# Linear attention before two feed-forward layers: k products on row halves, zero products in front, and two smaller edits in the first eight pairs

## The chip, the cores and the metric

The kernel runs on one core of one Trainium2 chip. The metric is the device time of one execution in microseconds (us); lower is better. Engines are called as in the profile: PE (TensorE products) and PEld (its weight loads), DVE (VectorE), ACT (ScalarE), POOL (GpSimd), SP (SyncE, which here only issues DMAs).

## The reference, cut to what matters

```python
def phi(x):
    proj = np.einsum('bhsd,df->bhsf', x, w_phi)
    proj = proj - np.max(np.abs(proj), axis=-1, keepdims=True)
    return np.concatenate([np.exp(proj), np.exp(-proj)], axis=-1)
q_p, k_p = (phi(q), phi(k))
kv = np.einsum('bhsf,bhsd->bhfd', k_p, v)
z = np.sum(k_p, axis=2)
num = np.einsum('bhsf,bhfd->bhsd', q_p, kv)
den = np.einsum('bhsf,bhf->bhs', q_p, z)[..., None] + 1e-06
attn = num / den
```

There are 4 batches, 8 heads, 576 positions, a head width of 64 and 128 features. The attention's output, 2304 tokens by 512, then goes through two feed-forward layers (512 to 2048 to 512), the first with a leaky ReLU and the second with SiLU.

## The kernel before, in words

Heads are worked in 16 pairs (4 for each batch). Head 0 of a pair lies on rows 0 to 63 of a tile, head 1 on rows 64 to 127. The first eight pairs (`full(i)`, `NFULL` = 8) use plain f32 products, the other eight split operands. Before the first feed-forward layer begins, the kernel does nearly all of the first eight pairs' work; the second eight are woven into that layer.

Steps of one of the first eight pairs, by line:

- L115 to L117 and L123: SP issues the loads of k (`kr`, 512 positions), of k's last 64 positions of both heads (`kt`), of q (`qr`) and of v (`va`).
- L180 (`s_pk(0)` and `s_pk(1)`): k times phi's weights. The 128 rows of a 128-position block of k are the weights in the array, and a block-diagonal matrix `BDF` (128 x 256) runs through it, so that one product gives both heads' 128 features. Each of the four blocks is one product, and each f32 product is two instructions with a weight load each: 8 instructions a pair. Two blocks fill one PSUM bank (`ps_a`, four of them).
- L156, L157 (`k_features`): DVE takes the largest absolute value of each of the four groups in a bank, and subtracts it. L166, L167: ACT takes exp of the negative (`ke[:, :, 1]`), and then, in place, exp (`ke[:, :, 0]`), once for the first bank (512 columns) and once for the second together with the tail (640).
- L195: the same product for the tail. L217: q's products, on row halves already: head j uses rows 64 j to 64 j + 63 of `qr` and of `wraw`, and writes to a bank of its own. ACT copies them out (L223, L225), POOL takes the largest absolute value over the partitions (L227).
- L262, L268 (`s_kv`): exp features times v, 18 products (36 instructions) into one bank, sign 0 first, then sign 1. ACT copies the sums out (L273, tile `KV`, one buffer).
- L302, L305: q's features times `KV`; DVE divides (L311 to L313); L316, L320: transposes; ACT and DVE split the result into `xh` and `xl` (L287, L126), the operands of the feed-forward layer (L533, L553).

`wc` holds `BDF` in columns 0 to 255, and `wraw` (w_phi on both row halves) and the identity in columns 256 to 511. ACT's queue issues it as two DMAs (L75), `BDF` first.

Beside this, the feed-forward weights come from 64-bit words: SP loads `raw` (L411; three buffers, and some loads held back until POOL has written a token of a given pair), ACT and DVE narrow and split it (L420 to L425, L429, L126), and the second matrix is stored again (L485). The written order comes from the table `OFF0` (a due time for each step of a pair) with five units between pairs. From it the framework plans the order on each engine, with its own estimates of durations; the order in the profile is not quite the written one. On the chip each engine then runs its instructions strictly in that order, SP's queue too.

Of the kernel before, what the change touches and what calls it, by code (L numbers as in the profile page):

```python
# [8 lines left out]
F32 = mybir.dt.float32  # L9
# [10 lines left out]
def tile_linear_attention_ffn_ffn(ctx: ExitStack, tc: tile.TileContext, q, k, v, w_phi, w_in1, w_out1, w_in2, w_out2, out):  # L20


    nc = tc.nc
    B, H, S, D = 4, 8, 576, 64
    F = (w_phi.shape[1] - 128) // 3
# [5 lines left out]
    S0 = 512  # L31
# [6 lines left out]
    NKV, NNUM = 112, 96  # L38
# [5 lines left out]
    gp = ctx.enter_context(tc.tile_pool(name="gp", bufs=2))  # L44
# [7 lines left out]
    def at(shape, dt, tag):  # L52
        return att_pool[0].tile(shape, dt, tag=tag, bufs=AB[0].get(tag, 1), name=tag)

    def ps(tag):

        return psp.tile([128, 512], F32, tag=tag, name=f"ps_{tag}")
# [3 lines left out]
    def aps(step):  # L61

        return ps("y" if PRO[0] and step in ("pq", "kv", "nt") else "a")
# [3 lines left out]
    BDF, wraw, ident = wc[:, 0 : 2 * F].rearrange("p (j f) -> p j f", j=2), wc[:, 2 * F : 3 * F], wc[:, 3 * F :]  # L67
# [5 lines left out]
    def make_consts():  # L73
        for c in (slice(0, 2 * F), slice(2 * F, 3 * F + 128)):
            nc.scalar.dma_start(wc[:, c], w_phi[:, c])  # L75
        first = [const.tile([128, 2], F32, name=f"first{i}") for i in range(2)]
        nc.gpsimd.memset(first[0], 0.0)
        nc.gpsimd.partition_all_reduce(first[1], first[0], 128, bass_isa.ReduceOp.absmax)
# [30 lines left out]
    def load_qk(i):  # L109

        st = P[i]
        st["kr"] = at([128, S0], F32, "kr")
        st["kt"] = at([128, 128], F32, "kt")
        st["qr"] = at([128, S], F32, "qr")
        nc.sync.dma_start(st["kr"], k[i, :, 0:S0])  # L115
        nc.sync.dma_start(st["kt"], k[i, :, S0:])
        nc.sync.dma_start(st["qr"], q[i])  # L117

# [6 lines left out]
    def sub(out_, x, h):  # L125
        nc.vector.tensor_tensor(out_, x, h.bitcast(F32), op=ALU.subtract)  # L126

    def full(i):
        return i < NFULL
# [21 lines left out]
    def k_features(i, pk, ng, g0):  # L151

        ke = P[i]["ke"]
        km = at([128, 4], F32, "km")
        src = pk[:, 0 : ng * F].rearrange("p (g f) -> p g f", f=F)
        nc.vector.tensor_reduce(km[:, 0:ng], src, op=ALU.max, axis=AX.X, apply_absolute_value=True)  # L156
        nc.vector.tensor_tensor(  # L157
            ke[:, g0 : g0 + ng, 0, :], src, km[:, 0:ng].unsqueeze(2).to_broadcast([128, ng, F]), op=ALU.subtract
        )
        g1 = g0 + ng  # L160
        if g1 == 8:
            return
        if g1 == 9:
            g0 = 4
        e0, e1 = ke[:, g0:g1, 0, :], ke[:, g0:g1, 1, :]
        nc.scalar.activation(e1, e0, AF.Exp, scale=-1.0)  # L166
        nc.scalar.activation(e0, e0, AF.Exp)  # L167

    def s_pk(c2):
        def f(i):  # L170
            st = P[i]
            if c2 == 0:
                st["ke"] = at([128, 9, 2, F], F32, "ke")
            pk = aps("pk")
            for u in range(2):
                c = 2 * c2 + u
                cs = slice(c * 128, (c + 1) * 128)
                o = pk[:, u * 2 * F : (u + 1) * 2 * F]
                if full(i):
                    nc.tensor.matmul(o, st["kr"][:, cs], BDF.rearrange("p j f -> p (j f)"), start=True, stop=True)  # L180
                    continue
                bh, bl = BDH.rearrange("p j f -> p (j f)"), BDL.rearrange("p j f -> p (j f)")
                nc.tensor.matmul(o, st["krh"][:, cs], bh, start=True, stop=False)
                nc.tensor.matmul(o, st["krl"][:, cs], bh, start=False, stop=False)
                nc.tensor.matmul(o, st["krh"][:, cs], bl, start=False, stop=True)
            k_features(i, pk, 4, 4 * c2)

        return f
# [67 lines left out]
    def s_kv(i):  # L256
        st = P[i]
        ke, va = st["ke"], st["va"]
        pv = aps("kv")[:, 0 : 4 * NKV].rearrange("p (s j d) -> p s j d", s=2, j=2)
        vf = va.rearrange("p c d -> p (c d)")  # L260
        for s in range(2):
            nc.tensor.matmul(  # L262
                pv[:, s, :, 0 : D + 1], ke[:, 8, s, :], va[:, 8:10], start=True, stop=False, skip_group_check=True
            )
            for j in range(2):
                for c in range(4):
                    w = (4 * j + c) * (D + 1)
                    nc.tensor.matmul(  # L268
                        pv[:, s, j], ke[:, 2 * c + j, s, :], vf[:, w : w + NKV], start=False, stop=(j == 1 and c == 3), skip_group_check=True
                    )  # L270
        if full(i):
            st["KV"] = at([128, 2, 2, NNUM], F32, "KV")
            nc.scalar.activation(st["KV"], pv[:, :, :, 0 : NNUM], AF.Copy)  # L273
            return
        h, l = st["KVH"], st["KVL"] = at([128, 2, 2, 2, D], F32R, "KVH"), at([128, 2, 2, 2, D], F32R, "KVL")
        for j in range(2):
            kv_, z_ = pv[:, :, j, 0:D], pv[:, :, j, D : D + 1].to_broadcast([128, 2, D])
            for slot, sr in ((j, kv_), (1 - j, z_)):
                nc.scalar.activation(h[:, j, :, slot, :], sr, AF.Copy)
                sub(l[:, j, :, slot, :], sr, h[:, j, :, slot, :])  # L280
# [80 lines left out]
    def s_num(a):  # L361
        return lambda i: (num_full if full(i) else num_split)(i, a)

    W, WP = 8.0, 5.0
    fns = dict(
        lq=load_qk, lv=load_v, sp=s_split, pq0=s_pq(0), pq1=s_pq(1),
        pk0=s_pk(0), pk1=s_pk(1), pkt=s_pkt, eq0=s_eq(0), eq1=s_eq(1), kv=s_kv, num0=s_num(0), num1=s_num(1), fin0=s_fin(0), fin1=s_fin(1),
    )
    FIN = 16
# [19 lines left out]
    def run_att(until, tile_=None):  # L389
        while seq and (seq[-1][0] < until or (tile_ is not None and missing(tile_))):  # L390
            if seq[-1][1] == NFULL and AB[0] is ABUFS0:
                att0_ctx.close()
                att_pool[0] = att_ctx.enter_context(tc.tile_pool(name="att1", bufs=1))
                AB[0] = ABUFS1
            _, i, n_ = seq.pop()
            f = fns[n_]
            f(i)
# [76 lines left out]
    def prep_wi(layer, c):  # L474
        raw = load_wi(layer, c)
        h = wp.tile([128, KD, 128], F32R, tag="wih", bufs=NC, name="wih")
        l = wp.tile([128, KD, 128], F32R, tag="wil", bufs=NC, name="wil")
        split64(raw, h.rearrange("p k f -> p (k f)"), l.rearrange("p k f -> p (k f)"))
        wi[layer, c] = (h, l)
# [235 lines left out]
    def pace(s):  # L715

        return SLOW * min(s, NC) + FAST * max(0, s - NC)

    make_consts()
    for c in range(PRE):  # L720
        run_att(13.52 + 11.07 * c)
        prep_wi(0, c)
# [52 lines left out]
    for u, gs in GROUPS.items():  # L775
        for i, ps_ in enumerate(gs):
# [7 lines left out]
            if last:  # L784
                y = y3_ops(u, list(ps_))
# [87 lines left out]
```

## Time and profile before

| | us |
|---|---|
| median of 3 runs | 964.19 (962.32 to 964.91) |
| the profiled execution's own time | 963.19 |
| its span, first to last instruction | 961.4 |
| PE busy | 943.6 (98%) |
| DVE busy | 649.1 (68%) |
| ACT busy | 597.2 (62%) |

The span is 1.8 us less than the profiled execution's time; the rest lies around it. A busy PE is one with some product in flight, so its share does not say how fast products follow each other. The clock column of the profile reads full speed from start to end.

### The profile page before, as it was taken

The numbers are of one execution on the slowest core, as the hardware profiler recorded it, in microseconds if no ns is written. First come the engines' busy times: TensorE is split into PE (matmuls) and PEld (weight loads), VectorE is DVE, ScalarE is ACT, GpSimd is POOL, SyncE is SP. The second block draws the span as 40 slices with busy tenths as digits, with TensorE's granted clock in tenths as the row PEclk, the third lists the DMA queues.
The fourth block names the chain that finished last, engine by engine and source line by source line (L and its number), as shares of the span: only waits on it lengthen the run. The fifth ranks groups of instructions, "written<-read, shape, count | busy, mean of one in ns | idle before, by whom it ended". The sixth has DMA issues, their size and how long they took to land.

```text
span 961.4 us, 15778 instructions
## 1 busy us (share of the span) xinstructions
PE 943.6 (98%) x5376; PEld 883.6 (92%) x5376; DVE 649.1 (68%) x1279; ACT 597.2 (62%) x1224; POOL 78.4 (8%) x56
## 2 busy tenths in 40 slices
PE   7999999999999999999999999999999999999998
PEld 6878888889999998888888999999999999999998
DVE  6677799986666655278777767778762595624853
ACT  6568687877777776466655556566554565544553
POOL 3434200201111111000000000000000000000000
PEclk9999999999999999999999999999999999999999
DMA  6333477874334232299999999896988778987784
GB/s 223 99 105 102 154 243 256 284 267 129 116 112 116 78 128 79 86 355 384 356 337 334 368 356 346 299 349 239 319 287 294 243 234 264 300 281 222 251 278 138
DMA packets 102384, 226.13 MB, mean 235 GB/s; under 512 B 15008, under 2 KB 24992, under 8 KB 102304
## 3 DMA queue, kind: packets, MB, share of 16 engines
q1 hardware_dynamic: 102016, 224.86, 69.9%
q8 instruction: 43, 0.70, 0.3%
q14 instruction: 37, 0.30, 0.1%
q10 hardware_dynamic: 288, 0.26, 0.1%
HBM read 177.82 MB, written 47.22 MB: 234 GB/s over the span
## 4 chain that ended last, share of the span: by engine, by line
PE 79%; DMA 8%; DVE 6%; ACT 4%; issue 1%; SPq 1%; DVEq 0%; ACTq 0%
PE ps_y L689 18%; PE ps_y L553 16%; PE ps_a L533 16%; PE ps_a L613 10%; PE ps_y L613 8%; DMA d<-rec 2%; PE ps_a L268 2%; PE ps_a L302 2%; DMA rec<-e 2%; PE ps_a L334 1%; PE ps_y L268 1%; DMA raw<-in_moe_w_in_dram 1%; DMA e<-d 1%; PE ps_a L180 1%; DMA w7s<-wst 1%
## 5 line engine op out<-in xcount | busy, mean ns | idle before, releaser
L689 PE MATMUL ps_y<-gt,ws 128*128 128x384 f32 x1008 | 177.2, 337 | 0.0
L689 PEld LDWEIGHTS ps_y<-gt,ws 128*128 128x128 f32 x1008 | 176.4, 188 | 0.1
L553 PE MATMUL ps_y<-gh,wo 128*128 128x460 f32 (+1 forms) x640 | 149.5, 372 | 2.2 <-DVE wo L126 1.3
L553 PEld LDWEIGHTS ps_y<-gh,wo 128*128 128x128 f32 x640 | 119.0, 188 | 16.6 <-ACT gh L429 1.9
L533 PE MATMUL ps_a<-xh,wih 128*128 128x460 f32 (+1 forms) x320 | 119.4, 373 | 0.8 <-ACT p L223 0.8
L533 PE MATMUL ps_a<-xl,wih 128*128 128x460 f32 (+1 forms) x320 | 118.9, 372 | 0.0
L533 PE MATMUL ps_a<-xh,wil 128*128 128x460 f32 (+1 forms) x320 | 118.7, 371 | 0.0
L613 PE MATMUL ps_a<-xs,ws 128*128 128x384 f32 x546 | 104.7, 338 | 0.1
L613 PEld LDWEIGHTS ps_a<-xs,ws 128*128 128x128 f32 x546 | 96.7, 188 | 0.8 <-issue 0.4
L227 POOL PARTITION_ALL_REDUCE m<-p x32 | 72.9, 2280 | 293.7 <-ACT p L223 212.4
L429 ACT ACTIVATE gt<-g 128x384 fp32r<-128x384 f32 x120 | 62.8, 524 | 51.3 <-PE ps_y L689 49.3
L126 DVE TENSOR_TENSOR gt<-g,gt 128x384 fp32r<-128x384 f32 x120 | 66.5, 555 | 34.4 <-ACT gt L429 33.5
L613 PE MATMUL ps_y<-xs,ws 128*128 128x384 f32 x462 | 88.5, 338 | 0.1
L613 PEld LDWEIGHTS ps_y<-xs,ws 128*128 128x128 f32 x462 | 81.7, 188 | 0.6 <-DVE g L589 0.5
L553 PE MATMUL ps_y<-gl,wo 128*128 128x460 f32 (+1 forms) x320 | 81.6, 372 | 0.0
L126 DVE TENSOR_TENSOR gl<-g,gh 128x460 fp32r<-128x460 f32 (+1 forms) x80 | 51.6, 646 | 30.6 <-ACT gh L429 26.1
L533 PEld LDWEIGHTS ps_a<-xh,wih 128*128 128x128 f32 x320 | 60.2, 188 | 7.4 <-ACT p L223 1.0
L553 PEld LDWEIGHTS ps_y<-gl,wo 128*128 128x128 f32 x320 | 60.2, 188 | 7.0
L536 ACT ACTIVATE g<-ps_a 128x460 f32<-128x460 f32 (+1 forms) x80 | 44.1, 552 | 35.9 <-PE ps_a L533 35.1
L533 PEld LDWEIGHTS ps_a<-xh,wil 128*128 128x128 f32 x320 | 60.1, 188 | 6.8
L533 PEld LDWEIGHTS ps_a<-xl,wih 128*128 128x128 f32 x320 | 60.2, 188 | 6.0
L429 ACT ACTIVATE gh<-g 128x460 fp32r<-128x460 f32 (+1 forms) x80 | 46.6, 584 | 8.1 <-PE ps_y L553 7.1
(142 smaller groups left out, 1552.3 us busy)
## 6 DMA issues: line engine op xcount, KB each, us to landing
ws<-w7s SPq DMA_DIRECT2D x336, 256.0 KB, 3.7
wo<-wos SPq DMA_DIRECT2D x64, 512.0 KB, 5.2
w7s<-wst SPq DMA_DIRECT2D x48, 512.0 KB, 6.0
raw<-in_moe_w_in_dram SPq DMA_DIRECT2D x32, 512.0 KB, 5.3
raw<-in_moe_w_out_dram SPq DMA_DIRECT2D x32, 512.0 KB, 5.8
wos<-wo SPq DMA_DIRECT2D x16, 512.0 KB, 4.3
va<-in_v_dram SPq DMA_DIRECT2D x16, 325.0 KB, 4.1
qr<-in_q_dram SPq DMA_DIRECT2D x16, 288.0 KB, 3.9
```

The source lines that it names most:

```text
L126: nc.vector.tensor_tensor(out_, x, h.bitcast(F32), op=ALU.subtract)
L180: nc.tensor.matmul(o, st["kr"][:, cs], BDF.rearrange("p j f -> p (j f)"), start=True, stop=True)
L227: nc.gpsimd.partition_all_reduce(m, p, 128, bass_isa.ReduceOp.absmax)
L268: nc.tensor.matmul(pv[:, s, j], ke[:, 2 * c + j, s, :], vf[:, w : w + NKV], start=False, stop=(j == 1 and c == 3), skip_group_check=True)
L302: nc.tensor.matmul(pb[:, w : w + NNUM], e[:, s, cs], KV[:, s, j], start=(s == 0), stop=(s == 1))
L334: nc.tensor.matmul(o, lhs, st[m, a][:, s, j * w : (j + 1) * w], start=(n == 0), stop=(n == 5))
L429: nc.scalar.activation(h, f, AF.Copy)
L533: nc.tensor.matmul(ph, a[:, kk, :], b_[:, kk, :], start=(m == 0), stop=(m == 3 * KD - 1))
L536: nc.scalar.activation(g, ph, AF.Prelu, alpha=0.01)
L553: nc.tensor.matmul(Y[t][d][:, 0:n], a[:, ds_], b_, start=(c == 0 and m == 0), stop=(c == NC - 1 and m == 1), skip_group_check=True)
L613: nc.tensor.matmul(bank[b_], w[:, a, kk], x[:, c, kk], start=(first and m == 0), stop=(m == 5), skip_group_check=True)
L689: nc.tensor.matmul(bank[b_][db], w[:, a, db], t[:, c], start=(first and p == 0 and m == 0), stop=(p == NP - 1 and m == 2), skip_group_chec ...
```

## The change

Four edits. (1) In the first eight pairs, k's products are made head by head on row halves: the weights are 64 rows of k, and `wraw`'s 64 rows (128 columns) run through, so that a pair takes 8 products (16 instructions and 16 weight loads) where it took 4 (8 and 8). A bank holds one head's four blocks instead of two blocks of both heads, and both banks are asked for before the first product. `k_features` then runs on both, one after the other; the index of `ke` in `s_kv` follows. (2) A zeroed tile and three products on it stand ahead of the attention. (3) The first pair's `kr` comes as two DMAs. (4) `s_kv` begins with sign 1, whose exp ACT writes first.

```diff
-        nc.sync.dma_start(st["kr"], k[i, :, 0:S0])
+        for c in (slice(0, 256), slice(256, S0)) if i == 0 else (slice(0, S0),):
+            nc.sync.dma_start(st["kr"][:, c], k[i, :, c])
...
+            if full(i):
+                if c2 == 0:
+                    pks = [aps("pk"), aps("pk")]
+                    for c in range(4):
+                        for j in range(2):
+                            r = slice(64 * j, 64 * j + 64)
+                            nc.tensor.matmul(
+                                pks[j][:, c * F : (c + 1) * F], st["kr"][r, c * 128 : (c + 1) * 128], wraw[r], start=True, stop=True
+                            )
+                    for j in range(2):
+                        k_features(i, pks[j], 4, 4 * j)
+                return
...
-                if full(i):
-                    nc.tensor.matmul(o, st["kr"][:, cs], BDF.rearrange("p j f -> p (j f)"), start=True, stop=True)
-                    continue
...
-        for s in range(2):
+        for s in (1, 0):
...
+                    g = 4 * j + c if full(i) else 2 * c + j
                     nc.tensor.matmul(
-                        pv[:, s, j], ke[:, 2 * c + j, s, :], vf[:, w : w + NKV], start=False, stop=(j == 1 and c == 3), skip_group_check=True
+                        pv[:, s, j], ke[:, g, s, :], vf[:, w : w + NKV], start=False, stop=(j == 1 and c == 3), skip_group_check=True
...
+    def wake():
+
+        z, bank = gp.tile([128, 256], F32, tag="g", name="z", bufs=2), ps("y")
+        nc.vector.memset(z, 0.0)
+        for _ in range(3):
+            nc.tensor.matmul(bank[:, 0:256], z[:, 0:128], z, start=True, stop=True)
+
     make_consts()
+    wake()
```

## Rows read from the trace of the kernel before

**Rows 1.** The page's part 1: busy us, share of the span, instructions.
```profile
PE 943.6 (98%) x5376; PEld 883.6 (92%) x5376; DVE 649.1 (68%) x1279; ACT 597.2 (62%) x1224; POOL 78.4 (8%) x56
```

**Rows 2.** Windows of the attention's stage: stretch, length, busy of each engine, PEclk, DMA share, GB/s.
```profile
0.00:18.20 18.20, 12.29 (x67) 9.80 (x67) 10.43 (x19) 11.09 (x23) 5.10 (x9) 1.00 0.81 276
18.20:72.00 53.80, 51.71 (x387) 44.39 (x387) 40.45 (x84) 34.84 (x80) 20.64 (x16) 1.00 0.33 97
72.00:98.50 26.50, 25.46 (x198) 21.97 (x196) 21.16 (x50) 20.71 (x47) 11.12 (x10) 1.00 0.30 100
```

**Rows 3.** Chain of work that ended last, 0 to 24 us: start, us, what.
```profile
0.72 3.54 DMA wc<-in_w_phi_dram
4.30 3.80 PE ps_a L180 x8
...
8.49 5.30 DMA raw<-in_moe_w_in_dram
...
13.81 0.68 ACT t L420
...
22.48 2.00 PE ps_a L302 x16
```

**Rows 4.** Timeline: start, us, engine, line, shapes, count [idle before, releaser].
```profile
0.72 0.39 SPq L115 DMA_DIRECT2D kr<-in_k_dram  x1
4.73 0.31 ACT L81 ACTIVATE WH<-wc 128x128 fp32r<-128x128 f32 x1
8.12 0.69 DVE L156 TENSOR_REDUCE km<-ps_a 128x4 f32<-128x512 f32 x1 [0.29 <-PE ps_a L180]
12.10 0.49 PE L262 MATMUL ps_y<-va,ke 128*128 128x130 f32 x2 [0.43 <-ACT ke L167]
17.63 0.49 ACT L273 ACTIVATE KV<-ps_y 128x384 f32<-128x384 f32 x1
18.17 2.02 PE L302 MATMUL ps_a<-KV,qh 128*128 128x96 f32 x16 [1.17 <-ACT KV L273]
90.22 0.41 PE L316 MATMUL ps_y<-wc,x 128*128 128x128 f32 x2 [0.80 <-DVE x L313]
104.99 0.49 PE L262 MATMUL ps_y<-va,ke 128*128 128x130 f32 x2 [0.36 <-ACT ke L167]
```

**Rows 5.** Chain of work that ended last, 25 to 50 us: PE's blocks.
```profile
25.17 0.74 PE ps_y L217 x4
...
30.11 0.63 PE ps_y L217 x4
...
33.58 1.73 PE ps_a L180 x8
...
36.27 0.42 PE ps_y L262 x2
36.69 1.77 PE ps_y L268 x16
38.46 0.24 PE ps_y L262 x2
...
46.39 0.87 PE ps_a L180 x4
...
47.73 1.06 PE ps_a L180 x4
```

**Rows 6.** Chain of work that ended last, 61 to 98.5 us.
```profile
61.10 0.17 DVE d L311
...
71.92 3.84 DMA raw<-in_moe_w_out_dram
...
83.65 4.34 DMA raw<-in_moe_w_in_dram
...
98.01 0.48 DVE x L313
```

**Rows 7.** Line 75, the two loads of `wc`: issue to landing.
```profile
DMA to landing us min/median/max: 3.5/3.6/3.6
```

## The prediction

> **What bounds the kernel now.** I read the page's totals first: PE is busy 98% of the span [rows 1], so time is won only where PE gets less work or waits less. All four edits lie in the stage of the first eight pairs, which ends where the feed-forward layer begins, near 112 us; so I cut it by windows next [rows 2]. The reader should see three different stretches. To 18.2 us PE works 12.29 us, and the DMA engines are 0.81 busy at 276 GB/s. To 72 us PE is busy 51.71 of 53.80. To 98.5 us it is busy 25.46 of 26.50, but DVE works 21.16 there. Then I followed the chain of waits to see which of them ends each stretch.
>
> To 22.5 us the chain is weights of phi, first k products, the load of `raw`, then ACT and DVE without a pause until PE's next block [rows 3]. ACT stands still until that load has landed at 13.79 (8.49 + 5.30); `KV`, behind it in ACT's order, comes at 17.63, and PE's block at 18.17 has waited 1.17 us for it [rows 4]. From 22.5 to 61 us the chain is nearly all PE; pieces of it are in [rows 5]. From 61.10 it leaves PE for DVE and ACT, goes through two loads of feed-forward weights, of which the second is issued only when the first has been worked through, and comes back from DVE at 98.01 + 0.48 [rows 6]. PE stays busy beside that, and shows once how close DVE is: 0.80 us at 90.22 [rows 4].
>
> **k products on row halves.** What goes is 8 instructions in 1.73 us, 0.216 each for 256 columns [rows 5]. What comes is 16 instructions of 128 columns, so 0.108 each by column count. The nearest row for products this short is v's: 16 in 1.77 us, 0.111 each, with a weight load apiece [rows 5]. Whether two row halves run beside each other is shown by q's products, which are laid out so already: four instructions of 256 columns take 0.63 us, of 320 columns 0.74 [rows 5]. One after the other they would take 4 x 0.216 = 0.86. As two steps of two they take 2 x 0.216 = 0.43 and 0.20 more; with 320 columns 2 x 0.27 = 0.54 and 0.20 more. So halves overlap, and 0.20 is what entering this layout costs. Leaving it costs the next block 0.18: the first two of a kv group take 0.42 behind q's products and 0.24 otherwise [rows 5]. The new block is therefore 0.20 + 8 x 0.111 + 0.18 = 1.27 us, 0.46 less than 1.73. Bounds: with no overlap 16 x 0.111 + 0.38 = 2.16, 0.43 more than now; next to q's products, where both changes of layout fall away, 0.89, so 0.84 less. I take 0.46, since pairs 2 to 7 have other products around k's now. In pairs 4 and 5 the eight instructions are cut in two by the transposes, 0.87 + 1.06 [rows 5]; asking for both banks at once makes them one block, and saves 0.66.
>
> A bank a head: DVE's first reduction of 0.69 us now starts when half of the products are done and the second waits for the rest (0.29 us in the first pair [rows 4]); afterwards both can start after 0.20 + 0.89 us instead of 0.87 and 1.73. DVE needs about 2.8 us for both halves either way (two reductions and two subtractions of 0.69), so this is 0.2 us later at one end and nothing on the path. The number and shapes of DVE's and ACT's instructions do not change.
>
> **The first pair and the zero products.** The 8 first products take 3.80 us where later ones take 1.73 [rows 3, 5]; the clock column reads 1.00 here too [rows 2], so I go by the durations, which fit half speed (1.2 against 2.4 GHz) in the first products PE does at all. Three zero products are six instructions of the same shape, 6 x 0.475 = 2.9 us at that speed, and one small DVE write ahead of them. They lie in PE's 4.30 us of waiting for `wc` [rows 3], so they cost nothing as long as `wc` lands after about 4 us. If they raise the clock, the first k block is some 1.1 to 1.3 us instead of 3.8.
>
> Against that, the new products read `wraw`, which is in the second load of `wc`: issued at 1.15 us and landing 3.5 to 3.6 us later [rows 7], so near 4.7; ACT's copy of it starts at 4.73 [rows 4]. PE starts 0.45 us later, and k in halves can't help, since k has landed by 4.3. The second half of k is one issue more on SP (0.39 [rows 4]), ahead of `kt`, q and v of this pair and all loads behind; the DMA engines are loaded through this stretch [rows 2], so I let it cost nothing; without that cover it is 0.4.
>
> What is that worth? PE reaches the second pair's k about 2 us earlier, but ACT still waits for `raw` at 13.79. That landing is set by the bytes queued ahead, not by PE. I expect one exp of pair 1 (0.52 to 0.6 us) to move ahead of that wait, and so 0.5 us at 18.17 [rows 4]. Bounds: nothing (or 0.45 later), and 1.17, all of PE's wait there.
>
> **Sign 1 first.** kv waits for the second exp at 12.10 (0.43) and at 104.99 (0.36) [rows 4]; with sign 1 first the exp that is needed ends one exp, over 0.6 us, earlier, and the other is needed only 18 products of 0.111 later. The first wait is covered by ACT's wait for `raw`; the second counts: 0.36.
>
> **The sum.** Pair 2's 0.46 at 20 us falls away, since PE is released at 22.48 by ACT and DVE [rows 3]. Pairs 3 and 4 count, 0.46 + 0.66 = 1.12. Pair 5's block is at 61 us, just where the chain leaves PE: I count half, 0.33. Pairs 6 and 7, at 75 and 87 us, only make PE wait longer for DVE [rows 6], so 0. With 0.5 from the start and 0.36 from the sign: 2.3 us. The profiled execution took 963.19, so 960.9; the median of the runs shown is 1.0 above it, and for it I forecast 964.19 - 2.3 = **961.9**, 0.24% less. A measurement of this kernel tells about 0.3% (2.9 us) from no change, so this is on the edge. Its own range, with the start between +0.45 and -1.17 and pair 5 whole or not at all: 960.9 to 963.2.
>
> **Rivals.**
> PE counts everywhere. For it: from 18.2 to 72 us PE is busy 96%, and the loads on the chain wait on an order that is planned anew for the changed program. Then 1.17 + 4 x 0.46 + 2 x 0.66 + 0.36 = 4.7 us, so 959.5; where k comes next to q in some pairs, up to 0.38 more for each. Against it: rows 6, 27 us without PE.
>
> Slower: the eight steps don't reach 0.111 us. A step with 16 instructions and 16 weight loads on halves is in no row; q's steps are twice as long, and v's have one weight load, not two at once. If the weights of a half can't be loaded under that half's own products, a step is load and product one after the other, 0.111 (v's step, which a load can't exceed) + 0.108 = 0.219, and the block is 8 x 0.219 + 0.38 = 2.13, 0.40 more than now. The change loses from a step of (1.73 - 0.38) / 8 = 0.169 on. With 0.40 in pairs 1 to 7 and 0.45 at the start: 0.45 + 7 x 0.40 = 3.25 us, so 967.4. Against it: q's four instructions have room for one exposed load only (0.20), not for two. By itself: the Trainium skill, "TensorE: Matmul & The Clock Gate", section "Part 3: Packing small matmuls", says that a weight load overlaps products in flight only where the row group differs; by that rule the slower time would come out, but on the full array v's 0.111 a step, load included, already disagrees with it.
>
> It does nothing: all of PE's savings are swallowed by ACT, DVE and loads, and only the 0.36 stays: 963.8, within 0.3%. For it: the chain is off PE for 22 + 37 of 112 us.
>
> **How the numbers follow.** Forecast 0.39, PE everywhere 0.37, does nothing 0.11, slower by the steps 0.09, and 0.04 for a newly planned order that costs elsewhere. Faster by over 0.3%: 0.37 and the forecast's lower end, 0.42. Within 0.3%: the rest of the forecast and "nothing", 0.45. Slower: 0.13. The range goes from 958.2, within the rival where PE counts everywhere, to 965.5; it leaves out the slower cases and the far end of the faster one, some 0.2.
>
> **What would show it.** In the timeline of the changed kernel: zero products done before 4 us; first k product near 4.7 (right: `wraw` gates); its 16 instructions within 1.3 us (the clock is up) or 2.2 (it is not). Later k blocks of about 1.27 us in the chain, in pairs of starts; 2.1 would be the slower rival. `raw` landing near 13.8 again, and PE's block after `KV` within 0.5 to 1.2 us of 18.17. PE waits for DVE between 75 and 98.5 growing by about a microsecond (forecast), or not (PE everywhere). First feed-forward product near 109.7 instead of 112, and all later stages shifted by as much. A shift that the feed-forward stages lose or add to would prove me wrong where I looked least.

## The result and the profile after

The changed kernel takes 977.35 us (median of 4 runs, 975.51 to 978.11) against 964.25 for the kernel before (962.32 to 964.91): a ratio of 1.0136, 95% interval 1.0116 to 1.0157. The forecast was 961.9, and the range ended at 965.5. The profiled execution took 977.40 with a span of 975.6, 14.2 more than the 961.4 of before.

Read the page's totals first, as before: PE's instructions and busy time, then the clock in 40 slices of 24 us.

```profile
PE 956.5 (98%) x5446; PEld 894.4 (92%) x5446; DVE 649.6 (67%) x1280; ACT 595.4 (61%) x1224; POOL 75.6 (8%) x56
...
PEclk9879999999999999999999999999999999999999
```

PE is as busy as before by its share [rows 1], although its k products are shorter; but the second and third slices are below full clock. So the windows of [rows 2] come next, of the changed kernel, and with them the two stretches in which its granted-clock record reads half.

```profile
0.00:18.20 18.20, 15.12 (x89) 12.25 (x90) 9.96 (x17) 11.41 (x24) 6.51 (x9) 1.00 0.80 269
18.20:72.00 53.80, 48.52 (x314) 40.81 (x315) 32.43 (x66) 26.82 (x60) 15.22 (x14) 0.81 0.26 78
72.00:98.50 26.50, 25.58 (x214) 22.11 (x213) 21.08 (x46) 18.46 (x43) 9.97 (x9) 1.00 0.31 97
...
24.00:30.80 6.80, 6.80 (x30) 5.51 (x29) 3.44 (x9) 4.73 (x12) 2.34 (x1) 0.50 0.15 43
51.30:65.00 13.70, 13.12 (x58) 10.74 (x56) 6.26 (x15) 6.39 (x16) 1.05 (x1) 0.50 0.29 85
```

The same two stretches of the kernel before:

```profile
24.00:30.80 6.80, 6.80 (x56) 5.75 (x55) 3.31 (x8) 3.73 (x10) 2.34 (x1) 1.00 0.22 62
51.30:65.00 13.70, 13.12 (x94) 10.82 (x92) 9.52 (x21) 8.65 (x20) 4.96 (x4) 1.00 0.31 89
```

In 20.5 us PE is busy 19.92 us in both kernels, with 88 instructions in the changed kernel and 150 in the kernel before. Half speed (1.2 GHz instead of 2.4) cannot be seen in a busy share; it shows in the clock column and in the counts. As an estimate, half of the 20.5 us, it accounts for some 10 us.

The first feed-forward product stands at 125.1 us (before 111.7), so 13.4 of the 14.2 us are lost in the first eight pairs. (The prediction places all four edits there; the fourth, sign 1 first, also changes the second eight pairs, and the other 0.8 us were not followed up.) Where in that stage? The timeline of the changed kernel, answering to [rows 4]:

```profile
1.17 2.93 PE L735 MATMUL ps_y<-z 128*128 128x256 f32 x6 [1.17 <-DVE z L733]
4.28 0.31 ACT L81 ACTIVATE WH<-wc 128x128 fp32r<-128x128 f32 x1 [0.20 <-DMA wc<-in_w_phi_dram]
...
17.50 0.49 ACT L284 ACTIVATE KV<-ps_y 128x384 f32<-128x384 f32 x1
18.05 2.02 PE L313 MATMUL ps_a<-KV,qh 128*128 128x96 f32 x16 [1.44 <-ACT KV L284]
18.29 0.68 DVE L436 CUSTOM_DVE_ANT_0 r<-t,r 128x1024 uint16<-128x1024 uint16 x1
...
19.96 0.68 DVE L127 TENSOR_TENSOR wil<-r,wih 128x512 fp32r<-128x512 f32 x1
20.26 1.16 PE L181 MATMUL ps_a<-wc,kr 64*128 64x128 f32 x16
20.57 0.68 DVE L436 CUSTOM_DVE_ANT_0 r<-t,r 128x1024 uint16<-128x1024 uint16 x1
21.44 1.42 DVE L249 TENSOR_TENSOR m<-p,m 128x512 f32<-128x512 f32 x2
22.89 0.74 ACT L253 ACTIVATE qh<-m 128x640 f32<-128x640 f32 x1 [0.91 <-DVE m L249]
23.68 0.46 PE L313 MATMUL ps_a<-KV,qh 128*128 128x96 f32 x2 [2.25 <-ACT qh L253]
...
50.32 2.85 PE L313 MATMUL ps_a<-KV,qh 128*128 128x96 f32 x16 [1.77 <-ACT KV L284]
```

Read it from the wait of 2.25 us backwards. PE's second numerator group waits 2.25 us for `qh`; `qh` waits for `m` (L249); and on DVE `m` stands behind the low part of the first `raw` piece (L127) and the narrowing of the second (L436), which no product needs before the feed-forward layer. In the order of before, DVE had put `m` ahead of both, and PE went on at 22.48:

```profile
18.75 0.82 DVE L239 TENSOR_TENSOR m<-p,m 128x640 f32<-128x640 f32 x1
...
21.07 0.68 DVE L425 CUSTOM_DVE_ANT_0 r<-t,r 128x1024 uint16<-128x1024 uint16 x1
...
22.48 2.00 PE L302 MATMUL ps_a<-KV,qh 128*128 128x96 f32 x16 [0.31 <-ACT wih L429]
```

The wait of 1.77 us is of the same kind: `KV` stands on ACT behind a conversion (`wih`) that has itself waited 2.05 us for DVE's L436. Right behind the two waits of 2.25 and 1.77 us the clock falls, at 24.0 and 51.3.

The k products became cheaper, as priced: a pair's sixteen instructions take 1.16 us to their last end. The starts of ACT's copies of `KV`, one a pair, show where time goes:

| pair | 0 | 1 | 2 | 3 | 4 | 5 | 6 | 7 |
|---|---|---|---|---|---|---|---|---|
| before | 17.63 | 30.15 | 43.57 | 58.49 | 72.31 | 84.27 | 97.92 | 109.41 |
| after | 17.50 | 35.48 | 49.80 | 71.17 | 85.22 | 97.76 | 111.71 | 122.74 |

At the first pair the changed kernel is ahead by 0.13. It loses 5.5 us between pairs 0 and 1 and 6.5 between 2 and 3, the two steps with a wait and a stretch at half speed in them, and little elsewhere.

Two things could be behind it. Either the edits themselves disturb PE (row halves or zero products), or the order does: the framework plans the order on every engine anew for each program, and any edit can make it choose another.

### The profile page after: what moved, and what is told of

It is laid out like the page before. It is cut to its first block, busy times and chain, and to the rows that moved or that the text cites. A ratio compares the mean times of both kernels' runs of the same rounds, so it can differ in the third digit from the quotient of the medians.

```text
span 975.6 us, 15916 instructions
## 1 busy us (share of the span) xinstructions
PE 956.5 (98%) x5446; PEld 894.4 (92%) x5446; DVE 649.6 (67%) x1280; ACT 595.4 (61%) x1224; POOL 75.6 (8%) x56
## 4 chain that ended last, share of the span: by engine, by line
PE 80%; ACT 6%; DMA 6%; DVE 5%; issue 1%; SPq 0%; ACTq 0%; DVEq 0%
PE ps_y L700 18%; PE ps_y L564 17%; PE ps_a L544 16%; PE ps_a L624 10%; PE ps_y L624 8%; PE ps_a L313 2%; PE ps_a L279 2%; PE ps_a L345 2%; PE ps_y L279 2%; DMA raw<-in_moe_w_out_dram 1%; DMA d<-rec 1%; PE ps_a L181 1%; DMA x<-o 1%; PE ps_y L227 1%; DMA w7s<-wst 1%
## 5 line engine op out<-in xcount | busy, mean ns | idle before, releaser
L237 POOL PARTITION_ALL_REDUCE m<-p x32 | 70.9, 2218 | 308.2 <-ACT p L233 80.6
L127 DVE TENSOR_TENSOR gt<-g,gt 128x384 fp32r<-128x384 f32 x120 | 66.5, 556 | 35.0 <-ACT gt L440 33.1
L127 DVE TENSOR_TENSOR gl<-g,gh 128x460 fp32r<-128x460 f32 (+1 forms) x80 | 50.9, 637 | 31.1 <-ACT gh L440 25.5
L547 ACT ACTIVATE g<-ps_a 128x460 f32<-128x460 f32 (+1 forms) x80 | 44.1, 551 | 34.5 <-PE ps_a L544 33.7
```

The lines of the kernel that those rows point to most:

```text
L237: nc.gpsimd.partition_all_reduce(m, p, 128, bass_isa.ReduceOp.absmax)
L547: nc.scalar.activation(g, ph, AF.Prelu, alpha=0.01)
```

## Experiments

**One edit undone each, and row halves alone.** From the changed kernel: k products as before (u_row), no zero products (u_wake), sign 0 first (u_sign). And the kernel before with row halves and nothing else (o_row). All with orders planned anew.

```diff
u_row   -  matmul(pks[j][..], st["kr"][r, c * 128 : (c + 1) * 128], wraw[r])
        +  matmul(o, st["kr"][:, cs], BDF)          # and g = 2 * c + j
u_wake  -  wake()
u_sign  -  for s in (1, 0):
        +  for s in range(2):
o_row   =  before, with the first edit of the diff alone
```

> The changed kernel with k's products as they were before (128 rows, BDF, two blocks a bank); zero products, k in halves and sign 1 first stay. Theory T1 (clock after idle): the half-speed stretches follow an idle time of PE of 1.7 us or more that the newly planned order makes, so this kernel, planned anew, has half speed between 18 and 112 us only if it also has such an idle time; without one it comes to 961 to 966 us. Rival R (the row halves themselves let the clock fall): no half speed after 18 us whatever PE waits, 961 to 966 us. Rival O (the order alone costs, the clock little): 966 to 975 us without half speed.

> The changed kernel without the zero products. T1: as for the row halves alone, half speed only behind long idle times of PE; the first k products at half speed as with the zero products, so the zero products are worth nothing, within 1 us, apart from the order. R: half speed in 18 to 72 us again, 970 to 978 us. Rival Z (the zero products upset the clock): full speed after 11 us, 960 to 966 us.

> The changed kernel with sign 0 first again in the products with v. T1: half speed only behind an idle time of PE of 1.7 us or more, time 961 to 978 us by how many there are. R: half speed in 18 to 72 us again, 970 to 978 us. O: clock at full and still 966 us or more.

> Before plus the row halves of k alone. T1: half speed only behind an idle time of PE of 1.7 us or more; with one such 968 to 978 us, without one 960 to 966 us. R: half speed in 18 to 72 us again, with or without such an idle time, 970 to 978 us. O: 966 to 978 us with the clock at full.

Measured, against 962.58 for the kernel before on that chip (2 runs of each, 3 of before): u_row 975.53 (ratio 1.0095 to 1.0170), u_wake 974.99 (1.0083 to 1.0170), u_sign 977.45 (1.0106 to 1.0198), o_row 980.57 (1.0137 to 1.0232). All four are slow; every theory that gave less than 970 us missed. None of the three edits, taken away, brings the time back. The half speed is there without row halves, too. In u_row:

```profile
16.88 0.80 PE L304 MATMUL ps_a<-KV,qh 128*128 128x96 f32 x5 [1.73 <-ACT KV L275]
...
103.70 1.17 PE L304 MATMUL ps_a<-KV,qh 128*128 128x96 f32 x4 [3.84 <-ACT KV L275]
```

and its windows, with the columns of [rows 2]:

```profile
17.80:21.20 3.40, 3.40 (x15) 3.22 (x15) 3.06 (x8) 0.68 (x2) 0.44 (x2) 0.50 0.02 5
103.10:116.70 13.60, 12.42 (x55) 10.71 (x56) 5.89 (x14) 7.88 (x19) 2.97 (x3) 0.50 0.33 118
```

And without zero products in u_wake (a wait of 6.43 us at 22.30, half speed from 18.6 to 28.8 and 107.3 to 117.5). So neither of the two by itself is the cause. Theory T1, half speed only behind a wait of 1.7 us or more, holds in these two kernels but not everywhere: in o_row the clock falls at 115.1 with waits of only 0.80 and 1.52 us near it, and waits of 2.23 us in o_row (at 75.08) and in u_sign (at 56.97) have no half speed behind them. What the four kernels share is a new order. Counted from the traces, by the longest sequence that stands in the same order in the kernel before, 71 to 75% (u_row, u_wake) and 63 to 67% (u_sign, o_row) of the first 160 instructions on DVE and on ACT are in line with it (the changed kernel: 84 and 80%).

**The order held, the edits in or out.** The orders of one kernel were written into another, as dependencies without semaphores between neighbours on an engine: they bind the planner and leave the chip nothing to wait for.

```python
row = [mine[r] for r in ranks]          # one engine's instructions, in the order to hold
for a, b in zip(row, row[1:]):
    tc.add_manual_dep(b, a.name, DependencyInfo(DependencyClass.NoSync, DependencyReason.DATA))
```

h_after has all four edits in the order of before. p_before has none, in the order of the changed kernel. h_stall is the kernel before in its own order, with one ACT copy done five times:

```diff
-            nc.scalar.activation(st["KV"], pv[:, :, :, 0 : NNUM], AF.Copy)
+            for _ in range(5 if i == 3 else 1):
+                nc.scalar.activation(st["KV"], pv[:, :, :, 0 : NNUM], AF.Copy)
```

> All four edits, but the instructions that both kernels have stand on every engine in the order of the kernel before (a block's eight row halves at the place of its first old product, zero products ahead of all, the second half of the first k right behind the first). Theory 'order' (the loss of 13 us comes from the newly planned order of ScalarE, VectorE and TensorE, whose waits let TensorE's clock fall to half): no stretch at half speed between 11 us and the end, first feed-forward product at 108 to 112 us (changed kernel 125.1), time 959 to 964 us, ratio 0.995 to 1.000. Theory 'row halves or zero products upset the clock by themselves': half speed for 3.4 to 13.7 us in the first eight pairs also in this order, first feed-forward product beyond 116 us, time 968 to 978 us. If the edits also save what the prediction priced (2.3 us), 961 us.

> None of the four edits, but the instructions stand in the order that was planned for the changed kernel. Theory 'order': as slow as the changed kernel, 972 to 979 us, ratio 1.009 to 1.017, with half speed in the first eight pairs and waits of TensorE of 1.5 us and more ahead of each fall. Theory 'row halves or zero products': near the kernel before, 961 to 967 us, full clock from 9 us on.

> The kernel before in its own order, with ScalarE's copy of KV of the fourth pair (0.49 us) done five times over in place of once, so that TensorE's first numerator product of that pair comes some 2 to 2.5 us late; nothing else is changed. Theory 'a wait of TensorE of about 1.8 to 2.3 us lets its clock fall': TensorE idles 1.8 to 3 us at that product, the granted clock falls to half within a microsecond or two and stays there for 3.4 to 13.7 us, time 2 us of the wait and 2 to 7 us of half speed over before: 966 to 973 us. Theory 'a wait costs itself alone': clock stays full, time 964.5 to 967 us.

| | median us | runs | ratio, 95% |
|---|---|---|---|
| before | 963.44 | 20 | |
| h_after | 964.24 | 10 | 1.0008 (0.9991 to 1.0024) |
| p_before | 969.03 | 3 | 1.0076 (1.0043 to 1.0108) |
| h_stall | 968.20 | 8 | 1.0051 (1.0035 to 1.0067) |

h_after: the whole loss is gone with the order, and the edits bring nothing that can be told from no change. Its expectation of full clock missed, though, and so did that of a first feed-forward product by 112 us (115.9): PE finishes its first products earlier, and then waits longer. The timeline of h_after, ACT's rows and PE's:

```profile
14.48 0.66 ACT L440 ACTIVATE t<-raw 128x512 f32<-128x512 f32 x1 [2.28 <-DMA raw<-in_moe_w_in_dram]
...
18.29 0.46 ACT L293 ACTIVATE KV<-ps_y 128x384 f32<-128x384 f32 x1
...
18.81 1.01 PE L322 MATMUL ps_a<-KV,qh 128*128 128x96 f32 x6 [3.18 <-ACT KV L293]
```

The window behind the wait:

```profile
19.50:26.30 6.80, 6.80 (x39) 6.35 (x39) 5.72 (x12) 3.79 (x6) 2.51 (x1) 0.50 0.13 33
```

ACT stands still until `raw` has landed, and seven instructions stand ahead of `KV` from there on, four of them conversions. PE's wait of 1.17 [rows 4] became 3.18, and half speed followed (and once more, from 94.6 to 98.0, behind a wait of 1.83 at 92.95). Half speed in this order was the sign of the other theory, that the edits themselves upset the clock; the same edits with the waits filled, in h_fill below, run at full clock, which speaks against it.

p_before: the order alone, without an edit, costs 5.6 us by the medians, less than expected (972 to 979 us) and less than half of what the changed kernel loses. In the profiled execution it does so at full clock:

```profile
core 0: 967.3 us, clock 1.000
```

by the view of the cores' clocks, and by the window of [rows 2]:

```profile
18.20:72.00 53.80, 48.14 (x345) 40.41 (x346) 38.53 (x80) 32.70 (x76) 15.98 (x14) 1.00 0.33 101
```

PE is busy 48.14 of 53.80 there, 3.6 us less than in [rows 2], and waits for ACT at the three places where the changed kernel does:

```profile
19.25 2.02 PE L311 MATMUL ps_a<-KV,qh 128*128 128x96 f32 x16 [1.39 <-ACT KV L282]
24.34 0.46 PE L311 MATMUL ps_a<-KV,qh 128*128 128x96 f32 x2 [1.09 <-ACT qh L252]
49.06 2.02 PE L311 MATMUL ps_a<-KV,qh 128*128 128x96 f32 x16 [1.56 <-ACT KV L282]
```

With the edits these waits are 1.44, 2.25 and 1.77 us: in the second, PE comes 1.8 us earlier and `qh` only 0.7. One of p_before's three runs took 974.86 with a mean granted clock of 0.994 instead of 1.000: the same program, with and without half speed.

h_stall: one wait, made on purpose in a kernel that is otherwise untouched.

```profile
61.18 2.24 PE L312 MATMUL ps_a<-KV,qh 128*128 128x96 f32 x9 [2.67 <-ACT KV L283]
```

and the window in which its clock record reads half; it begins before the wait has ended:

```profile
60.20:67.00 6.80, 5.82 (x23) 5.36 (x24) 1.91 (x7) 1.61 (x3) 0.00 (x0) 0.50 0.05 13
```

Expected were 1.8 to 3 us of wait, a fall, and 966 to 973 us; measured 2.67, the fall, and 968.2, all 8 runs at a mean clock of 0.994 to 0.998. The four extra copies are 4 x 0.49 = 2.0 us of ACT; the kernel lost 4.8. So this wait cost itself and then a stretch at half speed. The Trainium skill, "TensorE: Matmul & The Clock Gate", section "HAM oscillation — how this bites in real kernels", describes this for a load that PE waits for again and again; here the one wait of 2.67 us in an otherwise busy stage is enough.

**Waits filled with products that nobody needs.** If idling is what lets the clock fall, products of the identity by itself, put ahead of the waiting group into bank columns that are never read, should hold it. f_after is the changed kernel in its own order with 3, 6 and 5 of them ahead of the three waits; h_fill is h_after with 9 and 5 ahead of its two; h_fill2 has in addition the copy of the first pair's `KV` ahead of the second conversion, and 6 and 5.

```diff
+    def fill(bank, n, w):
+        for _ in range(n):
+            nc.tensor.matmul(bank[:, 512 - w : 512], ident, ident[:, 0:w], start=True, stop=True)
...
h_fill2 ACT:  t64, r64 (2nd raw), KV(0)  ->  KV(0), t64, r64
```

> The changed kernel in its own order, with products of the identity by itself (0.28 us each at full speed, into columns of a bank that nobody reads) put on TensorE in front of the three numerator groups ahead of which it sat idle for 1.44, 2.25 and 1.77 us: 3, 6 and 5 of them. Nothing that the kernel needs comes earlier by it. Theory 'idle stretches let the clock fall, and that is most of the loss': half speed at 24.0 to 30.8 us and 51.3 to 65.0 us goes away, which gives back up to 10 us, and what stays is the cost of the order at full clock: 967 to 970 us, as the kernel before in this order (969.0). Theory 'the clock falls for another reason than idling' (row halves, zero products): 975 to 978 us with half speed in the same places.

> All four edits in the order of the kernel before, with nine such products in front of the first numerator group of all (TensorE idle 3.18 us there) and five in front of the sixth pair's first transposes (idle 1.83 us). Theory 'the edits save what was priced, and the half speed after these two waits takes it back': no half speed between 11 us and the end, which gives back (6.8 + 3.4)/2 = 5.1 us of the profiled 965.7: 959 to 961.5 us, ratio 0.996 to 0.998. Theory 'the other engines swallow whatever TensorE saves': 963 to 965 us, ratio 0.999 to 1.001, with TensorE idling elsewhere. If the added products come late and hold TensorE up, above 965.

> The kernel with all four edits, the order of before and added products, with one instruction moved besides: ScalarE's copy of KV of the first pair goes ahead of the two conversions of the second raw piece that stand in front of it (0.65 us each), and six products are put before the first numerator group instead of nine. First numerator product at 17.6 to 17.9 us instead of 18.81. If the first pairs' chain sets the end, 0.8 to 1.1 us below the kernel with nine products: 958 to 960.5 us, ratio 0.995 to 0.998. If VectorE's and ScalarE's conversions set it, as that kernel or 0.5 us slower.

Against 964.07 for before (23 runs): f_after 972.84 (2 runs, 970.52 and 975.16; ratio 1.0053 to 1.0121), h_fill 963.40 (12 runs; 0.9979 to 1.0006), h_fill2 964.52 (12 runs; 0.9986 to 1.0013). In f_after the two stretches that were at half speed in the changed kernel run at full clock:

```profile
24.00:30.80 6.80, 6.80 (x56) 6.10 (x56) 4.65 (x10) 5.32 (x13) 2.34 (x1) 1.00 0.28 81
51.30:65.00 13.70, 12.54 (x94) 10.33 (x94) 9.89 (x19) 9.46 (x21) 4.95 (x4) 1.00 0.38 108
```

There are 150 instructions, as many as before, 12 of them fillers. The profiled run took 970.52, 6.9 less than the profiled run of the changed kernel, by nothing but useless work. It still has a shorter fall (18.2 to 21.6 us), beside a wait of 1.76 us at 17.97 that three fillers did not cover, and its other run took 975.16. So 967 to 970 us was missed, and the intervals of the two kernels' ratios just touch (1.0121 here, 1.0116 there): that filling the waits holds the clock is shown in these stretches, what it gives back in time is not settled by two runs.

In h_fill the profiled clock is full from 4.7 us to the end, which the fillers were meant to do, and still nothing is won:

```profile
14.42 0.70 PE L237 MATMUL ps_y<-qr,wc 64*128 64x256 f32 x4
15.05 2.27 PE L314 MATMUL ps_a<-wc 128*128 128x128 f32 x18
18.86 0.91 PE L329 MATMUL ps_a<-KV,qh 128*128 128x96 f32 x6 [1.53 <-ACT KV L294]
```

PE has done its q products by 15.1 (before, 17.0), fills 2.3 us and waits on. The k blocks came at their price, in the chain of waits of h_fill:

```profile
34.28 1.09 PE ps_a L191 x16
...
46.59 1.31 PE ps_a L191 x16
```

The expectation of 959 to 961.5 missed; the other one, 963 to 965 because ACT and DVE swallow the saving, held. h_fill2 moved the first group to 17.25, only to have the next one wait 2.43 us at 23.04, with half speed from 23.2 to 26.6: a miss.

**The orders of ACT and DVE rearranged by hand.** If the saving stops at ACT's order in the first pairs, it must appear once that order lets PE go on. In h_first (all edits, and the five products ahead of the sixth pair's transposes that h_fill has) and b_first (no edit, no such products), ACT does the first pair's `qh` and `KV` before the first `raw` piece, and the second piece's conversions go behind the second pair's features.

```diff
-  ACT: .. ke | t64, r64 (1st raw) | ke, qh | t64, r64 (2nd raw) | KV(0), p, wih, qh ..
+  ACT: .. ke | qh, ke, KV(0) | t64, r64 (1st raw) | qh, p, ke, qh, wih | t64, r64 (2nd raw) ..
-  DVE: .. ke | narrow (1st), narrow (2nd) up to t | m(0,1) | wil, r, ..
+  DVE: .. ke | m(0,1) | narrow (1st) | d, km, ke, x, m(1,0), .. | narrow (2nd) ..
```

> All four edits in the order of before (no added products ahead of the first numerator group, five ahead of the sixth pair's first transposes), with the first 37 instructions of ScalarE's order and 39 of VectorE's rearranged by hand: the first pair's qh and its KV go ahead of the first raw piece's conversions, the second row part of the first pair follows behind them, and the second raw piece's conversions go behind the second pair's features. Theory 'the edits' savings stop at waits for ScalarE and VectorE in the first pairs': first numerator product at 15 to 16 us instead of 18.86, no idle stretch of TensorE over 1.5 us, first feed-forward product at 107.5 to 110.5 us, time 958 to 962 us, ratio 0.995 to 0.999. Theory 'the conversions of raw pieces set the end of this stage whatever comes first': the start is earlier but the first feed-forward product comes at 111.5 to 113 us again, 963 to 965 us.

> None of the four edits, with the same rearranged orders of ScalarE and VectorE: what the rearrangement alone is worth. By TensorE's work the first pair's kv sums end some 1.2 us later than with the edits, so first numerator product at 16 to 17 us, first feed-forward product 1 to 2.3 us later than in the kernel with edits: 960 to 964 us. If the edits save nothing here either, within 0.5 us of that kernel.

Against 963.49 (30 runs): h_first 962.51 (12 runs; ratio 0.9991, 0.9978 to 1.0005), b_first 964.59 (11 runs; 1.0014, 1.0003 to 1.0024). The first numerator groups, of h_first and then of b_first, start without a wait:

```profile
15.91 0.80 PE L329 MATMUL ps_a<-KV,qh 128*128 128x96 f32 x5
```

```profile
17.49 1.24 PE L311 MATMUL ps_a<-KV,qh 128*128 128x96 f32 x9
```

Here the four edits are worth something: 962.51 - 964.59 = -2.1 us, or by the ratios 0.9991 / 1.0014 = 0.9977, with the two intervals combined -0.6 to -3.9 us. Their sum was priced at -2.3; in the order of before it was -0.7 (h_fill, 0.9979 to 1.0006, no difference shown). But the rearrangement itself does not help (b_first is 1.1 slower than before, and above the 960 to 964 expected), and the three microseconds that h_first is ahead of before at 24 us are gone by 35: the first feed-forward product comes at 112.2, as the theory of the conversions said. The clock has a part in this, too: the six of the 12 runs of h_first with a mean clock of 1.000 took 959.02 to 962.42, five at 0.996 took 964.06 to 966.15. Sorted so after the fact it is a hint and not a test.

**One edit at a time.** The three others alone, orders planned anew: zero products (o_wake), sign 1 first (o_sign), the first k in two transfers (o_half).

```diff
o_wake  +  wake()
o_sign  -  for s in range(2):
        +  for s in (1, 0):
o_half  -  nc.sync.dma_start(st["kr"], k[i, :, 0:S0])
        +  for c in (slice(0, 256), slice(256, S0)) if i == 0 else (slice(0, S0),):
        +      nc.sync.dma_start(st["kr"][:, c], k[i, :, c])
```

> The kernel before with the zero products alone, its order planned anew (the first 160 instructions of VectorE agree with the order of before by 94%, of ScalarE by 82%). Theory 'order': the time goes with waits of TensorE and half speed and not with the products: at 0 to 1 waits over 1.5 us 962 to 966 us, at two or more 967 to 978. Theory 'zero products upset the clock': half speed in the first pairs without such waits, 968 to 976 us.

> The kernel before with the negative sign first in the kv sums and nothing else, its order planned anew (the first 160 instructions agree with those of before by 83 to 89%). Theory 'order': as for the kernel with zero products alone, 962 to 966 us if TensorE waits over 1.5 us at most once, 967 to 978 us if it does twice or more. As an edit in itself it is worth at most the 0.4 us by which the first kv product waited.

> The kernel before with the first k in two transfers and nothing else, its order planned anew (99% of the first 160 instructions agree with those of before). Theory 'order': 962 to 965 us, ratio 0.998 to 1.002, full clock from about 9 us on. By the prediction the first k product would come up to 0.5 us earlier, which waits for wraw at 4.3 us instead.

| edit alone | in line with the order of before (first 160, DVE / ACT, counted as above) | us | ratio, 95% |
|---|---|---|---|
| k in halves (8 runs) | 99% / 99% | 962.98 | 0.9984 to 1.0006 |
| zero products (8) | 95% / 94% | 963.15 | 0.9983 to 1.0003 |
| sign 1 first (3) | 91% / 90% | 968.32 | 1.0031 to 1.0060 |
| row halves (2) | 63% / 63% | 980.57 | 1.0137 to 1.0232 |

The expectation of o_half, full clock from about 9 us on, missed once: 3.4 us at half speed at 188.4, beside a wait of 2.13 us in the feed-forward layer. The time goes with the order: the two kernels nearest to it cost nothing, the farthest most. o_sign exchanges two loops of equal length, worth 0.4 us at most, and costs 4.8. Its expectation, 962 to 966 us with a single long wait, missed; its trace has one such wait and one fall:

```profile
19.01 0.74 PE L303 MATMUL ps_a<-KV,qh 128*128 128x96 f32 x2 [2.07 <-ACT KV L274]
```

and from within that wait on:

```profile
18.50:25.30 6.80, 6.29 (x24) 5.84 (x25) 5.48 (x11) 4.49 (x9) 2.16 (x1) 0.50 0.05 13
```

**A last try at a faster version.** h_best is h_first with the second pair's `p`, features and `KV` on ACT, and the first pair's `xl` on DVE, moved ahead of the second piece's conversions as well, to take away a wait of 0.74 us at 28.62 behind which h_first fell to half speed in the profiled run (31.1 to 34.5); five other runs of the 12 have a lower mean clock still (0.996).

```diff
-  ACT: .. qh, wih | t64, r64 (2nd raw) | xh, ke, p, wih ..
+  ACT: .. qh, wih, xh, ke, p, ke, KV(1) | t64, r64 (2nd raw), wih ..
-  DVE: .. x | narrow (2nd) | xl, xl, xl, wil ..
+  DVE: .. x | xl | narrow (2nd) | xl, xl, wil ..
```

> The kernel with all four edits and the rearranged orders, rearranged once more: on ScalarE the second pair's p, last features and KV stand ahead of the second raw piece's conversions (before, its copy of wih waited 2.67 us at 28.27 us with KV behind it), on VectorE the first pair's xl stands ahead of that piece's conversions (TensorE idled 0.74 us for it at 28.62 us, and the clock was half from 31.1 to 34.5 us in the profiled run, as in 5 of 12 runs by their mean clock). If that wait lets the clock fall: no half speed in the first eight pairs, TensorE does the second pair's first numerator product at 28 to 29.5 us instead of 30.23, time 959.5 to 962 us, ratio 0.996 to 0.998. If the conversions of raw pieces set the end of the stage: first feed-forward product at 111 to 113 us and 962 to 964 us whatever the clock does.

It took 963.44 (12 runs; ratio 0.9983 to 1.0004, before 963.87): a miss. The wait was not removed, it moved and grew:

```profile
34.71 0.66 PE L344 MATMUL ps_y<-wc,x 128*128 128x128 f32 x2 [2.99 <-DVE x L340]
```

and with it:

```profile
33.90:40.70 6.80, 5.99 (x25) 4.83 (x26) 5.11 (x11) 5.88 (x14) 1.26 (x4) 0.50 0.38 124
```

No version tried here beats the kernel before by more than the measurement can tell.

## Why the prediction was wrong

**The step that failed** is the base from which the sum subtracts: 963.19 - 2.3 took the kernel before, changed the instructions that the diff names, and left everything else at its place. The text ahead of the prediction says that the framework plans the order with its own estimates, and the prediction names "a newly planned order that costs elsewhere", but gives it a chance of 0.04, no place and no price. Without that order the loss is not there (h_after). Its price, from the runs: the order alone 5.6 us at nearly full clock (p_before). The other 7.5 of the 13.1 us measured by the medians come where the new order and the edits meet: PE is ready earlier, waits longer, and 20.5 us at half speed follow, an estimated 10 us. With the edits' own -2.1 (h_first against b_first) that is 5.6 + 10 - 2.1 = 13.5. These three come from different programs, so the sum is a consistency and no proof of each part.

That the new order is needed for the loss, and costs without any edit, is shown in both directions: edits in, order of before, 0.9991 to 1.0024; edits out, order of after, 1.0043 to 1.0108. That the rest is half speed and nothing else is argued, not shown. Why the planner chooses this order is not shown either. That it puts conversions ahead of `m` and `KV` fits an order made from other durations than the chip's, but its estimates were not looked at.

**The second thing left out** is what a wait of PE costs. The prediction priced waits at their length, and used half speed only for the first products of all. h_stall lost 4.8 us by 2.0 us of ACT's work. Because of that, a gain in front of a wait can turn into a loss: PE ready earlier means PE idle longer (1.17 to 3.18 us in h_after).

**Point by point.**

- The k block: right. 0.20 + 8 x 0.111 = 1.09 us without the leaving term; in h_fill's chain it is 1.09 and, in the pair where it was cut in two, 1.31, where before had 1.73 and 0.87 + 1.06 [rows 5]. The transposes behind it take 0.37 there instead of 0.22, so leaving cost 0.15 where 0.18 was priced. The slower rival, a step of 0.219, is out. The Trainium skill, "TensorE: Matmul & The Clock Gate", section "Part 3: Packing small matmuls", would have given that step by its rule that a weight load overlaps products in flight only where the row group differs; the trace, with 1.09 us, does not agree.
- Zero products: half right. They ran from 1.17 to 4.10, hidden, and alone changed nothing (0.9983 to 1.0003). That they raise the clock was not reliable: the record reads full from 4.1 us (u_row) and 4.7 (h_fill), but only from 10.4 in the changed kernel, later than before's 8.6; its first k block took 2.1 us, that of h_fill 1.3.
- `wraw` gates the first k product: right; 4.39, behind `wc`'s second landing.
- `raw` pins the start near 13.8: half right. In the order of before it does, but 0.7 us later: ACT waits 2.28 us and takes it up at 14.48 in h_after, 13.81 before. In the changed kernel ACT does not wait for it: it is busy with exps, `qh` among them, up to 14.75, and `raw` has landed by 14.2. That only the bytes queued ahead set the landing was assumed; with an issue within 0.1 us of before's it comes as late as 14.88 in o_wake, and why is not shown.
- Pairs 2, 6 and 7 swallowed: right in kind and too weak. In before's order the copies of `KV` come 0.71, 0.70, 0.21, 0.22, 0.46, 0.20, 0.27 and 0.27 us later in h_fill than before: the start is later by 0.7 with the landing of `raw`, and only 0.4 to 0.5 us of the 1.45 counted for pairs 3 to 5 comes back.
- Sign 1 first, 0.36: the wait at 104.99 is gone with it (h_fill, h_first) and stands without it (b_first, 0.36 at 106.25). But nothing of it reaches the next step: from pair 6's copy of `KV` to pair 7's takes 11.49 us before and in h_fill alike. As an edit by itself it changed the order, for 4.8 us.
- "It does nothing" (0.11): what held the order came out so, within some 2 us either way.

## What to carry to other kernels

Where a planner orders the instructions, an edit has two effects, and the second, the new order, can be many times the first: compare the orders of the two programs before pricing the edit, and hold the old order when the edit is to be measured by itself. Price a wait of TensorE with the half speed that may follow it, and read the clock column and the instruction counts of a stretch beside its busy share. Work saved on one engine in front of a wait for another is not saved: ask which engine's order it will wait for next.

## What the runs showed of the hardware

In the first eight pairs, waits of PE of 2 to 3 us were mostly followed by half speed, for 3.4 to 6.8 us in the profile (2.07 in o_sign, 2.25 in the changed kernel, 2.43 in h_fill2, 2.67 in h_stall, 2.99 in h_best), but two of 2.23 us were not (o_row, u_sign). Of shorter waits, 1.73 (u_row), 1.76 (f_after) and 1.77 (the changed kernel) were; 1.17 (before), 1.39 and 1.56 (p_before), and 1.81 and 1.94 (o_row, at 24.09 and 64.24) were not, while h_first fell 2.5 us after a wait of only 0.74 that lay between products on row halves. So no length of a wait is safe or fatal by these runs. In h_stall, h_best and o_sign the record turns to half before the wait has ended. The same program can go either way (p_before, 969.03 at a mean clock of 1.000 and 974.86 at 0.994), which widens the spread of a kernel with such a wait: h_first 959.02 to 966.15 in 12 runs, the kernel before 961.66 to 965.45 in 30 beside it.
